# Loading the V cache in rows of 4 KB and the first weight in rows of 8 KB in a grouped-query decode attention kernel

**The chip, the cores and the metric.** The kernel runs on one core of a Trainium2 chip, with the other cores idle. The metric is the time of one execution on the device in microseconds; lower is better. A profiled execution also has a span, from its first to its last instruction, which is 1.7 to 3.0 us shorter than that execution's time in the runs of this case. Each run is classed as fast or slow by how far it lies above the fastest run of the same kernel; comparisons below use fast runs unless the text says otherwise.

## The reference, cut to what matters

```python
# x [32,1,512], k_cache and v_cache [32,8,2048,128], wq [512,4096], wo [4096,512], all bf16
W = 512                                            # only the last 512 keys count
q = (x @ wq) as [32, 32 heads, 1, 128]
k, v = the last W keys of each cache, each of 8 heads shared by 4 query heads
p = softmax(q @ k^T / sqrt(128)) ;  out = (p @ v) as [32, 4096] @ wo
```

Each of the 32 batch elements needs 1 MB of K and 1 MB of V, used once. With wq and wo, 4 MB each, 75.5 MB have to be read. A key of one head is 256 B, and the keys of a head follow each other in memory, so it is a choice of the kernel how many keys in a row go to one partition. The heads lie 512 KB apart, because the cache holds 2,048 keys of each.

## The kernel before

One queue issues all loads, in the order K0, wq, V0, K1, V1, ..., wo. A slot is a buffer for the K or the V of one batch element:

```python
def load_k(b):                 # 4 K slots; rows of 16 keys = 4 KB
    if b >= NK:
        sp.wait_ge(pe_T3, b - NK + 1)
    for h in range(2):
        sp.dma_start(
            K_sb[:, b % NK, h * 16 * DH:(h + 1) * 16 * DH],
            k_cache[b, 4 * h:4 * h + 4, SK - W:, :].rearrange("g (s r) d -> s g (r d)", s=32),
        ).then_inc(sem_k[b % NK][h], 16)

def load_v(b):                 # 12 V slots; rows of kt = 4 keys = 1 KB
    ...
    sp.dma_start(
        v_slot(b)[:, :, :],
        v_cache[b, :, SK - W:, :].rearrange("g (p kt) d -> p g (kt d)", kt=KT),
    ).then_inc(sem_v[b % NV], 16)
```

wq comes as four column blocks in rows of 2 KB, wo in rows of 1 KB. Per batch element TensorE transposes K in 32 pieces (line 253 of the kernel before), VectorE copies three quarters of the result out of PSUM, the memory that TensorE writes to (it evicts them), and ScalarE one, and eight products give the scores. Per four elements (a quad) there is one softmax, four transposes of P (line 283) and a burst of 128 products with V (line 303), in which 128 keys of one head are contracted with the four columns of that head:

```python
for g in range(G):
    for kt in range(KT):
        last = pe.matmul(
            QO_ps[:, j * 32 + 4 * g: j * 32 + 4 * g + 4],
            lhsT=v_slot(b)[:, g, kt * DH:(kt + 1) * DH],
            rhs=PT_sb[:, qq % 2, kt * 128 + prow(g, j): kt * 128 + prow(g, j) + 4],
            start=(kt == 0), stop=(kt == KT - 1), tile_position=(0, 0),
        )
```

At the end, 32 products with wo (line 332) are summed on four strips of the array, and one more product adds the strips.

## Time and profile before

| kernel before | |
|---|---|
| time | 216.6 us median of 3 runs (216.5 to 217.15) |
| span of the profiled run | 215.7 us (this run took 217.76 us, a little over the three) |
| busiest compute engine | TensorE, 149.2 us (69%) |
| queue of all loads | 99.4% of the 16 DMA engines' span |
| rate, 27 to 165 us | 376 GB/s |
| mean granted TensorE clock | 0.79 |

Read it like this: a queue that is never empty, and engines that are idle a third of the time, mean that bytes over rate set the time. The share of the DMA engines says only that they always have something in hand, not that they carry as much as they could (from 27 to 165 us it reads 1.06 at 376 GB/s here, and 1.03 at 408 after the change). The GB/s row tells how much.

### The profile page before, as it was taken

The numbers are of one execution on the slowest core, as the hardware profiler recorded it, in microseconds if no ns is written. First come the engines' busy times: TensorE is split into PE (matmuls) and PEld (weight loads), VectorE is DVE, ScalarE is ACT, GpSimd is POOL, SyncE is SP. The second block draws the span as 40 slices with busy tenths as digits, with TensorE's granted clock in tenths as the row PEclk, the third lists the DMA queues.
The fourth block names the chain that finished last, engine by engine and source line by source line (L and its number), as shares of the span: only waits on it lengthen the run. The fifth ranks groups of instructions, "written<-read, shape, count | busy, mean of one in ns | idle before, by whom it ended". The sixth has DMA issues, their size and how long they took to land.

```text
span 215.7 us, 5573 instructions
## 1 busy us (share of the span) xinstructions
PE 149.2 (69%) x2501; PEld 120.0 (56%) x2501; DVE 89.7 (42%) x141; ACT 46.3 (21%) x61; POOL 10.0 (5%) x45
## 2 busy tenths in 40 slices
PE   0175755648955897486948984689758795895672
PEld 0164635437843786376727953678438484783620
DVE  0044733460546154623463355515661366055112
ACT  2001120232113212320332031121331122213103
POOL 6000200000000000000000000000000000000000
PEclk9999596997598858985697679685997587859655
DMA  5999999999999999999999999999999999999910
GB/s 166 369 397 374 375 376 375 375 375 375 375 378 376 377 376 378 378 377 376 377 377 375 378 376 378 373 377 377 375 377 377 376 372 376 376 366 319 354 67 6
DMA packets 48886, 75.91 MB, mean 352 GB/s; under 512 B 1696, under 2 KB 38624, under 8 KB 48864
## 3 DMA queue, kind: packets, MB, share of 16 engines
q1 hardware_dynamic: 48864, 75.57, 99.4%
q8 instruction: 19, 0.31, 0.6%
q14 instruction: 3, 0.02, 0.0%
HBM read 75.53 MB, written 0.03 MB: 350 GB/s over the span
## 4 chain that ended last, share of the span: by engine, by line
DMA 41%; PE 34%; SPq 13%; issue 5%; ACT 4%; DVE 1%; DVEq 0%; ACTq 0%
DMA K_sb<-in_k_cache_dram 41%; PE KT_ps L253 18%; PE QO_ps L303 13%; SPq L138 10%; SPq L148 3%; ACT PT_sb L437 2%; PE KT_ps L332 2%; ACT KT_sb L420 2%; SPq L129 1%; PE S_ps L271 1%; DVE P_bf L379 0%; DVEq L43 0%; DVE oT_sb L387 0%; DVE maxv L369 0%; DVE X_sb L406 0%
## 5 line engine op out<-in xcount | busy, mean ns | idle before, releaser
L253 PE MATMUL KT_ps<-perm,K_sb 128*128 128x128 bf16 x1024 | 90.7, 266 | 39.5 <-DMA K_sb<-in_k_cache_dram 32.9
L253 PEld LDWEIGHTS KT_ps<-perm,K_sb 128*128 128x128 bf16 x1024 | 81.8, 123 | 56.1 <-DMA K_sb<-in_k_cache_dram 48.1
L363 DVE COPY KT_sb<-KT_ps 128x1024 bf16<-128x1024 bf16 x96 | 63.8, 690 | 50.2 <-PE KT_ps L253 49.0
L420 ACT ACTIVATE KT_sb<-KT_ps 128x1024 bf16<-128x1024 bf16 x32 | 32.8, 1024 | 148.7 <-PE KT_ps L253 148.7
L303 PEld LDWEIGHTS QO_ps<-PT_sb,V_sb 128*128 128x128 bf16 x768 | 20.3, 100 | 7.2 <-ACT PT_sb L437 7.2
L303 PE MATMUL QO_ps<-PT_sb,V_sb 128*128 128x4 bf16 x768 | 20.8, 165 | 4.4 <-ACT PT_sb L437 4.4
L271 PE MATMUL S_ps<-KT_sb,QBD 128*32 128x512 bf16 x256 | 23.3, 446 | 0.7 <-ACT KT_sb L420 0.7
L387 DVE CAST oT_sb<-QO_ps 128x128 bf16<-128x128 f32 x8 | 5.8, 719 | 40.3 <-PE QO_ps L303 40.3
L208 POOL COPY QBD<-QT_sb 128x32 bf16<-128x32 bf16 x32 | 6.3, 211 | 145.3 <-PE S_ps L271 128.2
L353 DVE CAST QT_sb<-QO_ps 128x512 bf16<-128x512 f32 x2 | 4.8, 2392 | 13.7 <-PE QO_ps L231 13.7
L231 PE MATMUL QO_ps<-xT_sb,big_sb 128*128 128x32 bf16 x128 | 4.0, 183 | 9.2 <-DMA big_sb<-in_wq_dram 9.2
L231 PEld LDWEIGHTS QO_ps<-xT_sb,big_sb 128*128 128x128 bf16 x128 | 3.8, 101 | 9.4 <-issue 7.4
L303 PEld LDWEIGHTS QO_ps<-PT_sb,big_sb 128*128 128x128 bf16 x256 | 6.8, 100 | 2.8 <-ACT PT_sb L437 2.8
L303 PE MATMUL QO_ps<-PT_sb,big_sb 128*128 128x4 bf16 x256 | 7.0, 165 | 1.8 <-ACT PT_sb L437 1.8
L271 PEld LDWEIGHTS S_ps<-KT_sb,QBD 128*32 128x32 bf16 x256 | 4.0, 98 | 5.4 <-issue 3.3
L369 DVE TENSOR_REDUCE maxv<-S_ps 128x1 f32<-128x512 f32 x8 | 5.5, 691 | 3.4 <-PE S_ps L271 3.4
L428 ACT ACTIVATE P_f<-S_ps,negmax 128x512 f32<-128x512 f32 x8 | 5.5, 687 | 4.5 <-DVE negmax L371 4.5
L379 DVE TENSOR_SCALAR P_bf<-P_f,recip 128x512 bf16<-128x512 f32 x8 | 5.9, 742 | 0.3
L283 PE MATMUL PT_ps<-ident,P_bf 128*128 128x128 bf16 x32 | 3.8, 255 | 2.8 <-DVE P_bf L379 2.8
L332 PE MATMUL KT_ps<-wo_sb,oT_sb 128*32 128x512 bf16 x32 | 4.2, 628 | 1.5 <-DVE oT_sb L387 0.8
L437 ACT ACTIVATE PT_sb<-PT_ps 128x512 bf16<-128x512 bf16 x8 | 4.7, 592 | 1.5 <-PE PT_ps L283 1.5
L283 PEld LDWEIGHTS PT_ps<-ident,P_bf 128*128 128x128 bf16 x32 | 2.7, 117 | 3.3 <-DVE P_bf L379 3.3
(27 smaller groups left out, 15.4 us busy)
## 6 DMA issues: line engine op xcount, KB each, us to landing
K_sb<-in_k_cache_dram SPq DMA_DIRECT2D x64, 512.0 KB, 11.2
V_sb<-in_v_cache_dram SPq DMA_DIRECT2D x24, 1024.0 KB, 11.8
big_sb<-in_v_cache_dram SPq DMA_DIRECT2D x8, 1024.0 KB, 11.7
big_sb<-in_wq_dram SPq DMA_DIRECT2D x4, 1024.0 KB, 10.7
wo_sb<-in_wo_dram SPq DMA_DIRECT2D x4, 1024.0 KB, 12.8
x_sb<-in_x_dram SPq DMA_DIRECT2D x1, 32.0 KB, 1.7
out_dram<-out_sb SPq DMA_DIRECT2D x1, 32.0 KB, 1.5
```

Source lines behind the costliest of these rows:

```text
L138: sp.dma_start(K_sb[:, b % NK, h * 16 * DH:(h + 1) * 16 * DH], k_cache[b, 4 * h:4 * h + 4, SK - W:, :].rearrange("g (s r) d -> s g (r d)", ...
L148: sp.dma_start(v_slot(b)[:, :, :], v_cache[b, :, SK - W:, :].rearrange("g (p kt) d -> p g (kt d)", kt=KT),).then_inc(sem_v[b % NV], 16)
L208: pool.tensor_copy(dst, src).then_inc(pool_qbd, 1)
L231: last = pe.matmul(QO_ps[:, hl * 32:(hl + 1) * 32], lhsT=wq_sb[:, kt, h * DH:(h + 1) * DH], rhs=xT_sb[:, kt, :], start=(kt == 0), stop=(kt ...
L253: last = pe.matmul(KT_ps[:, t, i * 128:(i + 1) * 128], lhsT=K_sb[:, b % NK, r * DH:(r + 1) * DH], rhs=perm[:, :, :], start=True, stop=True ...
L271: last = pe.matmul(S_ps[32 * (g % 4):32 * (g % 4) + 32, q % 2, :], lhsT=QBD[:, b % NQB, g, :], rhs=KT_sb[:, b % NKT, g // 4, :, g % 4, :], ...
L283: last = pe.matmul(PT_ps[:, kt * 128:(kt + 1) * 128], lhsT=P_bf[:, qq % 2, kt * 128:(kt + 1) * 128], rhs=ident[:, :], start=True, stop=Tru ...
L303: last = pe.matmul(QO_ps[:, j * 32 + 4 * g: j * 32 + 4 * g + 4], lhsT=v_slot(b)[:, g, kt * DH:(kt + 1) * DH], rhs=PT_sb[:, qq % 2, kt * 12 ...
L332: last = pe.matmul(KT_ps[:, c, :].bitcast(F32)[32 * c:32 * (c + 1), :], lhsT=oT_sb[:, h, :], rhs=wo_sb[:, h, :], start=(h < 4), stop=(h >= ...
L363: dve.tensor_copy(KT_sb[:, b % NKT, t // 2, 8 * (t % 2):8 * (t % 2) + 8, :, :], KT_ps[:, t, :]).then_inc(dve_T, 1)
L420: act.activation(KT_sb[:, b % NKT, t // 2, 8 * (t % 2):8 * (t % 2) + 8, :, :], KT_ps[:, t, :], ACTF.Copy).then_inc(act_T, 1)
L437: act.activation(PT_sb[:, qq % 2, :], PT_ps[:, 0:512], ACTF.Copy).then_inc(act_PT, 1)
```

## The change

The intent is to load V in rows of 4 KB too, and wq in rows of 8 KB. V then lies in the array like K: partition (s, g) holds 16 keys of key block s of head g, so four heads share one 128-row operand. P has to follow: the softmax is written into a zeroed tile in which the probabilities of a head stand only where its partitions are (block-diagonal), so that one product contracts 32 key blocks times four heads. It costs 16 transposes of P per quad in place of four, and four strided writes on VectorE in place of one. The diff, cut to its core:

```diff
-    NK = 4
-    NV = 12
+    NK = 6
+    NV = 8
+    LEAD = 5
+    PVLAG = 6
 ...
+        def cache_rows(cache, b, h):
+            return cache[b, 4 * h:4 * h + 4, SK - W:, :].rearrange("g (s r) d -> s g (r d)", s=NS)
 ...
+            for kt in range(DKT):
+                sp.dma_start(wq_sb[:, kt, :], wq[kt * P:(kt + 1) * P, :]).then_inc(sem_wq[kt], 16)
 ...
             def load_v(b):
                 if b >= NV:
-                    sp.wait_ge(pe_PV, quad_of(b - NV) + 1)
 ...
+                    sp.wait_ge(pe_PV, b - NV + 1)
+                for h in range(2):
+                    sp.dma_start(
+                        V_sb[:, b % NV, h].rearrange("p r d -> p (r d)"), cache_rows(v_cache, b, h)
+                    ).then_inc(sem_v[b % NV], 16)
+
+            for b in range(B + LEAD):
+                if b < B:
+                    load_k(b)
+                if b >= LEAD:
+                    load_v(b - LEAD)
 ...
-                    v_cache[b, :, SK - W:, :].rearrange("g (p kt) d -> p g (kt d)", kt=KT),
 ...
+                for c in range(G4):
+                    rows = slice(32 * c, 32 * c + 32)
+                    dve.tensor_scalar(
+                        P_ex[rows, :, :, c], P_f32[rows, :].rearrange("p (r s) -> p r s", r=NR),
+                        recip[rows, q:q + 1], None, op0=ALU.mult,
+                    ).then_inc(dve_P, 1)
 ...
+                for h in range(2):
+                    r0 = score_row(h, j)
+                    for r in range(NR):
+                        ins = pe.matmul(
+                            QO_ps[:, 16 * h:16 * h + 16],
+                            lhsT=V_sb[:, b % NV, h, r, :],
+                            rhs=PT_sb[:, q % 2, r, :].rearrange("p (c n) -> p c n", c=G4)[:, :, r0:r0 + 4],
+                            start=(r == 0), stop=(r == NR - 1), tile_position=(0, 0),
+                        )
```

The scores and P in f32 have one buffer in place of two, wo takes wq's place in memory, and V's products are done per element, six elements behind K. wq now comes before K0 in the queue.

## The prediction

> **What bounds the kernel now.** I read the page from the top, then the queue's own numbers, then the memory rate in chosen stretches, then the end of the chain. The first two parts of the page already name the bound.
>
> ```profile
> PE 149.2 (69%) x2501; PEld 120.0 (56%) x2501; DVE 89.7 (42%) x141; ACT 46.3 (21%) x61; POOL 10.0 (5%) x45
> ...
> PEclk9999596997598858985697679685997587859655
> DMA  5999999999999999999999999999999999999910
> GB/s 166 369 397 374 375 376 375 375 375 375 375 378 376 377 376 378 378 377 376 377 377 375 378 376 378 373 377 377 375 377 377 376 372 376 376 366 319 354 67 6
> DMA packets 48886, 75.91 MB, mean 352 GB/s; under 512 B 1696, under 2 KB 38624, under 8 KB 48864
> ...
> q1 hardware_dynamic: 48864, 75.57, 99.4%
> ```
>
> No compute engine is over 70% busy, while the 16 DMA engines read 9 in every slice from the second to the one before the tail. The rate is flat at 375 GB/s, and it has one hump, 397, in the slice in which mostly wq arrives. 75.57 MB have to come in whatever the order; the time is their number divided by the rate, plus a start and a tail. The packet line says how they come: nearly 38,600 of the 48,886 packets are under 2 KB. These are V (32 MB in 1 KB rows) and wo (4 MB in 1 KB rows); K comes in 4 KB rows, wq in 2 KB rows.
>
> Next question: does the row size matter, or is 375 what memory gives? The stretches' view (columns: stretch, its length, busy time of five engines, TensorE clock, DMA share, GB/s):
>
> ```profile
> 9.00:15.00 6.00, 3.25 (x78) 3.18 (x79) 1.16 (x1) 0.00 (x0) 0.00 (x0) 1.00 1.04 396
> 27.00:192.00 165.00, 123.50 (x2077) 101.21 (x2074) 74.67 (x122) 37.95 (x50) 5.07 (x24) 0.79 1.06 376
> 195.00:204.00 9.00, 4.82 (x122) 3.59 (x120) 3.23 (x7) 2.40 (x4) 0.00 (x0) 0.87 1.06 340
> ```
>
> With the DMA share at 1.04 to 1.06 in all three, the rate is 396 with wq in flight (2 KB), 376 with K and V mixed (half 4 KB, half 1 KB) and 340 with wo nearly alone (1 KB). To separate K from V in the middle I counted in the trace's packet records how many 1 KB and 4 KB packets start in each microsecond of 27 to 192 us and fitted a time per packet to each size: 2.93 ns for 1 KB and 10.17 ns for 4 KB, so 350 and 403 GB/s for the core. Half and half that gives 2/(1/350+1/403) = 375, the rate shown. So row size is what costs.
>
> Does compute limit it anywhere? The waits of TensorE (who waited for what, total us, times, longest us):
>
> ```profile
> PE KT_ps L253 <- DMA K_sb<-in_k_cache_dram: 32.9, 24, 3.4
> PE QO_ps L231 <- DMA big_sb<-in_wq_dram: 9.2, 3, 7.4
> PE QO_ps L303 <- ACT PT_sb L437: 6.2, 8, 0.9
> ```
>
> TensorE waits for K, not the reverse. The chain also has 9.6% at the K issues waiting for a free K slot, but as the queue stays full behind that wait, it is back-pressure and costs nothing. The end:
>
> ```profile
> 205.39 0.72 DVE oT_sb L387
> 206.16 0.62 PE KT_ps L332 x3
> 206.77 0.66 issue
> 207.43 3.61 PE KT_ps L332 x29
> 211.07 0.68 DVE X_sb L406
> ```
>
> The last softmax, transposes and 128 PV products (201.8 to 205.4) are done just before the last wo packet. In the packet records the full stream falls off at 204.6 us, but some of the 16 engines lag and the last wo byte lands at 208.4. From the last wo product (211.05) to the end of the span (215.7) it is 4.65 us.
>
> [...] the clock in the trace is indeed 0.50 or 1.00 in every stretch short enough to hold one state. [...] the 128 PV products with 4 columns took 3.47 us in the chain, 27 ns each, so 16 columns in place of 4 should be free.
>
> **The change, part by part.**
> 1. V in 4 KB rows (the core). 33.55 MB at 403 in place of 350 GB/s: 95.9 us become 83.3, so -12.6 us on the path, since the queue is the bound. It is the largest term.
> 2. wq in 8 KB rows, and first in the queue. 4.19 MB at 394 (fitted for 2 KB) becomes at least 403: -0.2 us. The projection moves later: the last quarter of wq lands at about 13 us, TensorE then does 32 products (1.0 us for 32 in the trace). Copies of the result and the first transposes finish by about 20 us. Six K slots and V0, 7 MB or 18 us of transfers, are already issued by then, so the queue should not run dry.
> 3. wo stays in 1 KB rows, in wq's place: 12.4 us at the 337 seen (mean rate for wo), unchanged. It waits for the projection, long done.
> 4. K has 6 slots in place of 4, V 8, freed one at a time; V's load lags by 5 and PV by 6. A K load needs the transposes of the batch element six earlier, at which point about five K and five V blocks (10 MB) are outstanding. No gap in the queue; no gain either, as it had none.
> 5. Compute per batch element. TensorE at full clock: 32 transposes (16 took 1.08 us) 2.16, 8 score products 0.62, 32 PV products 0.87, and 16 instead of 4 transposes of P per quad (1.08/4) 0.27: 3.9 us. At half clock 3.45 + 1.04 + 0.87 + 0.43 = 5.8 us. The transfer of 2.10 MB at 403 takes 5.2 us. VectorE: three evictions of 0.69, 2.07; max, negation and reciprocal (0.69+0.15+0.16)/4 = 0.25; four normalisations on 32 partitions with a stride, estimated at the 0.74 of the present one, 0.74; one small copy, estimated 0.15: 3.2 us. ScalarE: 1.02, plus (0.88 + 2 x 1.02)/4: 1.75 us. All lie beside the transfers.
> 6. The tail. V31 lands a whole wo before the end, 12 us early; softmax and PV end before wo does. All but the last eight wo products run as wo arrives; the trace has four in 0.43 us, so eight and the semaphore are about 1.0 us after the last byte, against 2.65 now (208.4 to 211.05): -1.6 us.
>
> Sum, built up: first bytes at 2.3 us; wq 10.4; K and V 67.11 MB at 403, 166.5; wo 12.4: the mean engine ends at 191.6. The same sum for before, 2.6 + 10.6 + 83.3 + 95.9 + 12.4 = 204.8, meets the observed 204.6. Slowest engine +3.5 (before: 3.8): 195.1. Eight products 1.0, then 4.65: a span of 200.8. The measured time is 0.9 over the span (216.6 against 215.7): 201.7. [...] I take 200.6.
>
> **Rivals.**
> a) TensorE becomes the bound. For: at half clock it needs 5.8 us a batch element against 5.2 for the transfers, and the mean granted clock before is 0.79. Against: [...] five elements of prefetch absorb a slow spell. Even at half clock all through, 32 x 5.8 + about 16 + a tail of 7 makes some 209.
> b) The 4 KB gain is not there when all the rows have the same 512 KB pitch between heads: 403 was fitted with V's 1 KB rows beside. Against it speaks that K's half has that pitch already. If the whole stream stayed at 376, the tail and wq alone would save 2 us: some 214.
> c) The single score buffer, the single P buffer and the order on VectorE stall TensorE: four normalisations (about 3 us) stand between evictions once per quad. TensorE has 1.3 us of slack per element and the lag of 6; I see no chain longer than a period: 200 to 203.
> d) The uneven engines: [...] the slowest may end later than +3.5: up to 204.
>
> **Range and chances.** The transfer sum matched before within 0.2 us, so the error is the 4 KB rate (395 to 410, -3 to +4 us) and the tail (2 us either way): 196.5 to 205.5. Faster by over 2% means under 212.3, which only rival b) in full prevents: 0.95; within 2% 0.03; slower 0.02, for a stall I don't see.
>
> **What would show it.** DMA share at 9 throughout, and the rate at 400 or more in the middle slices in place of 376; packets near 23,000, with those under 2 KB near 5,900; TensorE still waiting on K, clock above 0.79; PV products near 27 ns apart; the chain ending in wo's landing, eight products and the same 4.65 us. The prediction is wrong if slices fall below 390, if zeros appear in the DMA row, or if the chain runs through VectorE's normalisation or TensorE without DMA.

Its sum comes to a span of 200.8 us and a time of 201.7. A term for a faster stream of 4 KB rows alone followed, and the 1.1 us between 201.7 and the forecast of 200.6 were taken off for it. That 16 columns cost no more than 4 keeps a ground in the trace before: its products with 4 columns start 26 ns apart (median), and those with 32 columns in the projection (line 231) also 26.

## The result, and the profile after

The changed kernel takes 200.39 us (median of 4 runs, 200.34 to 200.56) against 216.88 us (216.5 to 217.87) in the runs beside it, and it is correct. A ratio here is the mean time of one kernel's fast runs over that of the other's in the same rounds, so it is not quite the ratio of the medians: 0.9235, with a 95% interval of 0.9201 to 0.9268. The span of the profiled runs fell from 215.7 to 198.7 us, by 17.0; the medians differ by 16.5, as the profiled run of the kernel before was one of its longer ones.

The page of the changed kernel, with the busy time of the engines, the slices, and the first queue:

```profile
PE 142.8 (72%) x2597; PEld 111.8 (56%) x2597; DVE 100.8 (51%) x188; ACT 58.3 (29%) x70; POOL 13.3 (7%) x46
...
PEclk9999999699999969988998799969996797855555
DMA  5999999999999999999999999999999999999930
GB/s 181 424 418 411 409 407 412 403 411 407 408 411 403 409 407 407 410 407 409 406 407 410 407 413 403 408 407 407 411 406 411 401 409 406 410 396 334 344 133 7
DMA packets 23289, 75.95 MB, mean 382 GB/s; under 512 B 2208, under 2 KB 6368, under 8 KB 22752
```

The DMA row reads 9 as before, but the same row now stands for 401 to 413 GB/s in the middle and not for 375. The packets have halved. VectorE has become busier (51%), ScalarE too, and neither matters. Two stretches (same columns as in the prediction) show the rates of the two row sizes, wq at the start and K with V in the middle:

```profile
5.00:14.00 9.00, 3.56 (x113) 3.27 (x114) 0.00 (x0) 0.00 (x0) 1.30 (x4) 1.00 1.01 422
27.00:165.00 138.00, 109.44 (x2021) 86.69 (x2019) 84.36 (x157) 47.69 (x56) 6.01 (x22) 0.91 1.03 408
```

What TensorE waited for (total us, times, longest us):

```profile
PE KT_ps L236 <- DMA K_sb<-in_k_cache_dram: 22.4, 32, 1.6
PE PT_ps L268 <- DVE P_ex L359: 10.6, 6, 3.1
PE PT_ps L214 <- DMA w_sb<-in_wq_dram: 7.6, 4, 3.4
PE KT_ps L308 <- DMA w_sb<-in_wo_dram: 6.0, 4, 1.9
```

It still waits for K, now 32 short times, and for wo at the end. The second line is new: the block-diagonal writes hold up the transposes of P. Whether that costs anything can't be read from this view alone; an experiment below asks. The end of the chain:

```profile
181.61 11.21 DMA w_sb<-in_wo_dram
...
192.86 1.11 PE KT_ps L308 x8
...
194.00 0.68 DVE X_sb L382
```

Before, the chain reached wo's products through VectorE's copy of the last quad and did 32 of them in a row. Now it comes straight from the last wo transfer, and eight products are left.

The packet records (every packet of a trace, with its start, duration and size) give the span's bookkeeping, by when so many bytes had landed:

| stretch | before | after | gain |
|---|---|---|---|
| until 4.3 MB have landed (wq, some K) | 14.31 us | 13.08 us | 1.23 |
| the next 67.1 MB (about K and V) | 178.44 | 164.43 | 14.01 |
| until the last byte of wo | 15.64 | 14.85 | 0.79 |
| from there to the last product of wo | 2.66 | 1.61 | 1.05 |
| from there to the end of the span | 4.65 | 4.73 | -0.08 |
| sum | 215.7 | 198.7 | 17.0 |

### The profile page after: what moved, and what is told of

The parts are those of the page before. It is cut to its first block, busy times and chain, and to the rows that moved or that the text cites. A ratio compares the mean times of both kernels' runs of the same rounds, so it can differ in the third digit from the quotient of the medians.

```text
span 198.7 us, 5891 instructions
## 1 busy us (share of the span) xinstructions
PE 142.8 (72%) x2597; PEld 111.8 (56%) x2597; DVE 100.8 (51%) x188; ACT 58.3 (29%) x70; POOL 13.3 (7%) x46
## 4 chain that ended last, share of the span: by engine, by line
SPq 50%; DMA 28%; PE 14%; DVE 3%; issue 2%; ACT 1%; DVEq 0%
SPq L132 24%; DMA K_sb<-in_k_cache_dram 23%; SPq L140 18%; PE KT_ps L236 9%; SPq L151 7%; DMA w_sb<-in_wo_dram 6%; PE S_ps L253 2%; DVE P_ex L359 2%; PE QO_ps L286 1%; SPq L126 1%; DVE KT_sb L337 1%; PE PT_ps L268 1%; PE KT_ps L308 1%; ACT P_f L407 0%; DVEq L45 0%
## 5 line engine op out<-in xcount | busy, mean ns | idle before, releaser
L236 PE MATMUL KT_ps<-perm,K_sb 128*128 128x128 bf16 x1024 | 75.8, 238 | 22.6 <-DMA K_sb<-in_k_cache_dram 22.4
L236 PEld LDWEIGHTS KT_ps<-perm,K_sb 128*128 128x128 bf16 x1024 | 67.0, 107 | 29.2 <-DMA K_sb<-in_k_cache_dram 26.7
L286 PEld LDWEIGHTS QO_ps<-PT_sb,V_sb 128*128 128x128 bf16 x1024 | 28.2, 98 | 17.4 <-issue 13.9
L286 PE MATMUL QO_ps<-PT_sb,V_sb 128*128 128x16 bf16 x1024 | 31.2, 171 | 2.4 <-ACT PT_sb L417 1.2
L359 DVE TENSOR_SCALAR P_ex<-P_f,recip 32x512 bf16<-32x512 f32 x32 | 25.3, 791 | 1.1
L417 ACT ACTIVATE PT_sb<-PT_ps 128x1024 bf16<-128x1024 bf16 x16 | 15.5, 1021 | 19.1 <-PE PT_ps L268 19.1
L268 PE MATMUL PT_ps<-ident,P_ex 128*128 128x128 bf16 x128 | 9.7, 236 | 10.6 <-DVE P_ex L359 10.6
L268 PEld LDWEIGHTS PT_ps<-ident,P_ex 128*128 128x128 bf16 x128 | 8.2, 106 | 11.5 <-DVE P_ex L359 11.5
L366 DVE CAST oT_sb<-QO_ps 128x32 bf16<-128x32 f32 x32 | 5.9, 183 | 9.5 <-PE QO_ps L286 9.4
L308 PE MATMUL KT_ps<-w_sb,oT_sb 128*32 128x512 bf16 x32 | 4.3, 637 | 6.0 <-DMA w_sb<-in_wo_dram 6.0
```

The costliest lines, as they stand in the source:

```text
L236: ins = pe.matmul(KT_ps[:, t, i * 128:(i + 1) * 128], lhsT=K_sb[:, b % NK, h, 8 * (t % 2) + i, :], rhs=perm[:, :, :], start=True, stop=Tru ...
L268: ins = pe.matmul(PT_ps[:, r // 8, (r % 8) * 128:(r % 8 + 1) * 128], lhsT=P_ex[:, r, :, :].rearrange("p s g -> p (s g)"), rhs=ident[:, :], ...
L286: ins = pe.matmul(QO_ps[:, 16 * h:16 * h + 16], lhsT=V_sb[:, b % NV, h, r, :], rhs=PT_sb[:, q % 2, r, :].rearrange("p (c n) -> p c n", c=G ...
L359: dve.tensor_scalar(P_ex[rows, :, :, c], P_f32[rows, :].rearrange("p (r s) -> p r s", r=NR), recip[rows, q:q + 1], None, op0=ALU.mult,).th ...
L417: act.activation(PT_sb[:, q % 2, 8 * i:8 * i + 8, :].rearrange("p r n -> p (r n)"), PT_ps[:, i, :], ACTF.Copy,).then_inc(act_PT, 1)
```

## The experiments

All twelve ran on chips with the kernel before beside them. Five were made to ask about the gain, two about the tail, and five about whether rows can be made longer still, a question that the 422 GB/s of wq raised.

**Undo V's rows alone.** V is loaded as before, and the result is wrong:

```diff
-                for h in range(2):
-                    sp.dma_start(... cache_rows(v_cache, b, h)).then_inc(sem_v[b % NV], 16)
+                sp.dma_start(
+                    V_sb[:, b % NV].rearrange("p h r d -> p (h r d)").rearrange("p (g x) -> p g x", g=G),
+                    v_cache[b, :, SK - W:, :].rearrange("g (p kt) d -> p g (kt d)", kt=4),
+                ).then_inc(sem_v[b % NV], 16)
```

> The changed kernel with one part undone: V is loaded as in the kernel before, one transfer of 1 MB in 1 KB rows (the result is wrong on purpose, since the key order no longer matches). Theory (the row size of V is the gain): 33.55 MB at 350 in place of 408 GB/s cost 13.6 us, so 214 us, with the middle of the run at 376 GB/s. Rival (the gain comes from six K slots, the lag and the new order of work): within 2 us of 200.4. Mixed: in between, in proportion.

Measured: 214.47 us (214.36 to 214.53). The middle of this run, in the stretches' view:

```profile
27.00:165.00 138.00, 104.98 (x1856) 83.61 (x1856) 77.02 (x144) 43.67 (x52) 5.71 (x22) 0.89 1.06 376
```

The rate is back at 376 GB/s with all of the new slots, lag and order of work in place. The rival falls.

**V's rows alone, in the kernel before.** The other direction, wrong too:

```diff
-                sp.dma_start(v_slot(b)[:, :, :],
-                    v_cache[b, :, SK - W:, :].rearrange("g (p kt) d -> p g (kt d)", kt=KT))
+                for h in range(2):
+                    sp.dma_start(
+                        v_slot(b).rearrange("p g f -> p (g f)")[:, h * 2048:(h + 1) * 2048],
+                        v_cache[b, 4 * h:4 * h + 4, SK - W:, :].rearrange("g (s r) d -> s g (r d)", s=32))
```

> The kernel before with the one part alone: V loaded in 4 KB rows by two transfers of 512 KB (wrong on purpose, the products of V are those of the kernel before). Theory: 13.6 us less than 216.9, so 203, with 408 GB/s in the middle. Rival (the four K slots and the bursts of 128 products of the kernel before can't keep a faster stream fed): over 208, with the rate in the middle under 395.

Measured: 203.35 us (203.12 to 204.44), ratio 0.9363. The middle:

```profile
27.00:165.00 138.00, 111.01 (x1842) 90.11 (x1839) 65.99 (x108) 34.17 (x45) 5.03 (x24) 0.78 1.03 408
```

The old compute, with four K slots, feeds the faster stream just as well. So the way in which V is loaded accounts for 14.0 us of the span when taken away from the new kernel (212.7 against 198.7) and 14.2 when given to the old one (215.7 against 201.5); in median times it is 14.1 both ways. The 2.8 us of span that are left between this kernel and the changed one come from its start (0.95 us, by when 4.3 MB have landed) and its tail: its last product of wo ends 3.48 us after wo's last byte, and the changed kernel's 1.61.

Both runs change the order of V's addresses and the number of its transfers together with the row size, so the order could be a rival. Two records speak for the row size itself. The run with wq in 1 KB rows, below, leaves the addresses in memory as they are. And in the packet records of these kernels the most common duration of a packet is 46 ns for 1 KB (V before, wo), 84 for 2 KB (wq before), 159 for 4 KB (K, and V after) and 309 for 8 KB (wq after). These four lie on one line: 37.6 ns for every KB and 8.4 ns for each packet. Four packets of 1 KB thus take 1.16 times as long as one of 4 KB.

**Four K slots in place of six.**

```diff
-    NK = 6
+    NK = 4
```

> The changed kernel with four K slots in place of six, all else unchanged and the result right. Theory (depth has no part in the gain): within 0.6 us of 200.4. Rival (depth keeps the queue full): 203 or more, with gaps in the rate.

Measured: 200.49 us (200.46 to 200.52), correct; the span is 198.6. The depth of the K buffer has no part in the gain.

**wq in 1 KB rows.**

```diff
-                sp.dma_start(wq_sb[:, kt, :], wq[kt * P:(kt + 1) * P, :])
+                sp.dma_start(
+                    w_sb[:, 8 * kt:8 * kt + 8, 0:D], wq[kt * P:(kt + 1) * P, :].rearrange("p (a n) -> p a n", a=8))
```

(w_sb becomes 32 rows of 528 elements, so that pieces of 1 KB don't touch.)

> The changed kernel with wq in 1 KB rows (weights held in a padded tile, so that a row of wq falls into eight pieces), result right. Theory (the rate follows the row size for every input and the queue is the bound from the first byte): 4.19 MB at 350 in place of 424 GB/s, 2.1 us more, 202.5. Rival (the start is not on the path, as compute has to catch up anyhow): within 0.5 us of 200.4.

Measured: 202.63 us (202.51 to 202.78), correct, span 200.9. The start of this run:

```profile
5.00:14.00 9.00, 3.08 (x96) 2.79 (x96) 0.00 (x0) 0.00 (x0) 1.29 (x4) 1.00 1.09 361
```

361 GB/s in place of 422, and the 2.2 us of span that it costs stay in the sum to the end. The start is on the path. Only the length of the pieces differs here on the side of memory, and 422 over 361 is 1.17, as 408 over the fitted 350 for V is.

**Compute alone.** K and V are loaded until the slots are full, and then used again (wrong):

```diff
                 if b >= NK:
-                    sp.wait_ge(pe_T[3], b - NK + 1)
+                    return
 ...
                 if b >= NV:
-                    sp.wait_ge(pe_PV, b - NV + 1)
+                    return
```

> The changed kernel with only the first six K and eight V blocks loaded and then used again and again, so the transfers end early and all compute stays (wrong on purpose). Theory (transfers bound the kernel, compute has slack): 14 us of start, 32 elements at about 4 to 4.6 us and a tail of some 20 us: 160 to 180. Rival (TensorE or VectorE are within a few per cent of the bound too): 190 or more.

Measured: 171.44 us median; the runs are 169.53 to 172.27. TensorE's waits begin with:

```profile
PE PT_ps L268 <- DVE P_ex L359: 15.3, 8, 3.1
```

So the block-diagonal writes do stall TensorE, once in every quad, by 15.3 us in all, and this is part of what compute needs. But compute needs about 170 us in all, 30 below the changed kernel; this run's own loads were over after about 63 us. An element takes 4.2 us in it (1,623 products from 60 to 150 us, at 32+32+8+4 = 76 per element), and a transfer of 2.10 MB at 408 GB/s takes 5.1. The stall lies beside the transfers: V's rows alone in the kernel before, without these writes, gave the same 408 GB/s.

**The tail: V last.** All of wo is loaded before the last four V blocks:

```diff
             for b in range(B + LEAD):
 ...
+                for c in {24: [0], 25: [1], 26: [2], 27: [3]}.get(b - LEAD, []):
+                    load_wo(c)
```

> The changed kernel with all of wo loaded before the last four V blocks, so V31 lands last; result right. Theory (the tail behind the last byte is on the path): PV of the last element 1.0, its copy 0.2 and 32 products of wo at 1.07 per eight, 5.5 us in place of 1.6 behind the last byte: 3.9 more, less what the freer queue gives, 202.5 to 204.5. Rival (the tail does not matter): 200.4 within 0.5.

Measured: 205.82 us (205.16 to 206.05), correct: above the range that I had expected. The chain's end shows the mechanism:

```profile
193.23 1.02 PE QO_ps L289 x32
...
194.52 3.66 PE KT_ps L311 x32
```

V's last byte landed at 192.61 us and the last product of wo ended at 198.18, 5.6 us behind it in place of 1.6. The span, 202.7, is 4.0 us over that of the changed kernel, as the tail says. The time is 2.5 to 3.0 us above the span here, against 1.7 to 1.8 for the changed kernel, and that is what took it over the range. The kernel before (1.8 to 3.0 in the rounds of the experiments, mostly over 2.4) and the run with V's rows alone (2.5 to 2.9) have this too; what the three share is not shown.

**wo spread among the last V loads.** As above, with `{27: [0], 29: [1], 31: [2, 3]}`.

> The changed kernel with wo's first two loads moved between the last V loads (after V27 and V29), two left at the end; result right. In the changed kernel the issue of wo's last two transfers waits 12 us and the rate falls to 308 GB/s with a DMA share of 0.94 there. Theory (fast engines run dry while the issue waits for room): 1 to 2 us less, 199. Rival (1 KB rows and the slowest engine set the time wherever wo lies): 200.4 within 0.5.

Measured: 200.32 us (200.01 to 200.55), ratio 0.9203, interval 0.9175 to 0.9232, correct. The theory falls. From 180 to 190 us the rate is now 349 GB/s, but the last byte of wo lands at 192.32 us, and in the changed kernel it was 192.36. The bytes of wo merely moved; the last of them lands when it did. This is the nearest that any run came to beating the changed kernel, and it does not.

**Longer rows: K and V in 8 KB rows.** wq had shown 422 GB/s, so I tried 8 KB for all, with one transfer of 1 MB each (wrong):

```diff
-                        K_sb[...], cache_rows(k_cache, b, h)            # [32 blocks][4 heads][4 KB], twice
+                    K_sb[:, b % NK].rearrange("p h r d -> p (h r d)"),  # [16 blocks][8 heads][8 KB], once
+                    k_cache[b, :, SK - W:, :].rearrange("g (s r) d -> s g (r d)", s=16),
```

> The changed kernel with K and V each loaded by one transfer of 1 MB in 8 KB rows (wrong on purpose). Theory (a fixed cost per row): wq's stretch in 8 KB rows showed 424 GB/s, so 67.1 MB go from 164.5 to 158.3 us and the time to 194. Rival (4 KB is already at the ceiling and wq's 424 only showed a fresh queue): within 1 us of 200.4.

Measured: 317.54 us (307.05 to 318.93). Both expectations were far off. The DMA and GB/s rows of its page:

```profile
DMA  7999999999999999999999999999999999999990
GB/s 278 354 222 224 226 225 225 225 224 226 230 230 230 230 226 228 233 230 234 231 240 238 254 257 261 259 267 258 260 249 263 274 266 253 254 249 231 242 317 24
```

The engines are as busy as ever, at 222 to 274 GB/s in the middle. Four more kernels changed one thing of the pattern each. All vary by several per cent from run to run, and the lowest run stands in the table. The rates of the five slow patterns are those of the profiled runs; the gap to 408 GB/s is far larger than the differences among runs of a kernel.

| blocks x heads x row of a transfer | blocks taken together | lowest run | GB/s, 50 to 150 us |
|---|---|---|---|
| 32 x 4 x 4 KB (the changed kernel) | all | 200.34 us | 408 |
| 16 x 8 x 8 KB | all | 307.05 | 229 |
| 16 x 4 x 8 KB, on 64 partitions | all | 305.51 | 228 |
| 16 x 8 x 4 KB | every other | 282.42 | 244 |
| 16 x 8 x 4 KB | adjacent ones | 263.95 | 250 |
| 16 x 4 x 4 KB, on 64 partitions | adjacent ones | 296.05 | 255 |

The edits and expectations, in that order. Four heads in rows of 8 KB:

```diff
-            return cache[b, 4 * h:4 * h + 4, SK - W:, :].rearrange("g (s r) d -> s g (r d)", s=NS)
+            return cache[b, 4 * h:4 * h + 4, SK - W:, :].rearrange("g (s r) d -> s g (r d)", s=16)
```

> K and V in 8 KB rows again, but each 512 KB transfer fills 64 partitions from 16 blocks of four heads in place of 128 partitions from 16 blocks of eight (wrong on purpose). Theory A (a row of 8 KB out of heads that lie 512 KB apart is slow in itself): near 317 us and 225 to 245 GB/s as with eight heads. Theory B (the eight heads of the pattern did it): 200 us or less.

Median 312.87 us: not the eight heads alone. Rows of 4 KB in the pattern of the slow run:

```diff
+            return cache[b, :, SK - W:, :].rearrange("g (s h r) d -> h s g (r d)", s=16, h=2)[h]
```

> K and V in 4 KB rows, but fetched in the pattern of the slow 8 KB run: each 512 KB transfer takes the first or second half of 16 blocks of all eight heads, 8 KB apart (wrong on purpose). Theory A (row length of 8 KB): about 200 us with 400 GB/s or more. Theory B (pattern of eight heads at 512 KB distance): over 250 us.

Median 295.1 us: not the row length alone. Adjacent blocks in place of every other one:

```diff
+            return cache[b, :, SK - W:, :].rearrange("g (h s r) d -> h s g (r d)", s=16, h=2)[h]
```

> As the slow run in 4 KB rows of eight heads, with one difference: a transfer takes 16 blocks that follow each other in memory (the first or the second half of a head's window) in place of every other block (wrong on purpose). Theory (blocks fetched side by side that leave every other 4 KB out are what is slow): about 200 us and 400 GB/s or more. Rival (eight heads in one transfer are what is slow): 280 us or more, as before.

Median 281.14 us: not the gaps, or not they alone. The last one is correct and puts the same bytes in the same places in rows of 4 KB; each transfer of the changed kernel is only cut in two:

```diff
+            for i in range(2):
+                sp.dma_start(
+                    K_sb[64 * i:64 * i + 64, b % NK, h].rearrange("p r d -> p (r d)"),
+                    cache_rows(k_cache, b, h, i))      # keys 256*i to 256*i + 255, s=16
```

> The changed kernel with each 512 KB transfer of K and V cut into two of 256 KB, over the first and the last 16 blocks of the same four heads: rows of 4 KB, the same bytes in the same places, result right. All four slow patterns so far had 16 blocks per transfer. Theory A (16 blocks per head in a transfer are what is slow): 260 us or more. Theory B (eight heads side by side, or 8 KB rows of four heads, are what is slow): 200 to 204, the extra being eight issues of about 0.6 us per element in a period of 5.1.

Median 305.49 us (296.05 to 306.09), as theory A expected:

```profile
DMA  6999999999999999999999999999999999999990
GB/s 267 376 241 242 243 245 251 248 262 259 260 262 253 256 248 250 251 258 259 259 259 263 255 248 246 248 245 245 240 240 240 241 243 247 253 248 246 297 309 13
```

The queue is full throughout, so the doubled number of issues is not what holds it up. The packet records show where the time goes: from 50 to 150 us a packet of 4 KB takes 262 ns (median) in place of 161 in the changed kernel, while wq's packets of 8 KB take 309 ns as ever. What the five slow patterns share is an outermost dimension of 16 on the side of memory, where the fast loads have 32 (K, V) or 128 (wq, the old V). That is a correlation over five kernels. The profile doesn't name the engine that carried a packet. Why a packet of such a transfer takes longer stays open, and so does what 8 KB rows of the caches would give in a pattern with more blocks.

## Why the prediction was right, point by point

The time was predicted as 200.6 us, with a range of 196.5 to 205.5; it is 200.39. The mechanism and the place of the bound were right. The figure was closer than its terms, some of which erred in opposite directions, so part of its closeness is luck (see "From span to time").

- **V's rows (step 1).** Predicted -12.6 us; both experiments say -14, in either direction. The fit to the mixed stream had put 4 KB at 403 GB/s, and the stream runs at 408 once all of it is in 4 KB rows, so K gained a little as well (the median packet of 4 KB from 27 to 165 us took 164 ns before and 161 after). K and V took 164.4 us in place of the 166.5 of the sum.
- **wq (step 2).** Predicted -0.2 us, taken with a cautious "at least 403" for 8 KB. It is mis-sized: the start gained 1.23 us, because 8 KB rows gave 422 against 392 to 396 GB/s in 2 KB rows, and the first row starts 0.4 us earlier (2.23 us against 2.61). That the queue would not run dry behind the later projection held: no slice dips.
- **wo (step 3).** The stretch was to be unchanged at 12.4 us plus 3.5 for the slowest engine. It took 14.85 in place of 15.9.
- **Depth (step 4).** No gain, as said; the run with four slots shows it.
- **Compute (step 5).** Beside the transfers, as said. The estimates were 3.9 us per element for TensorE at full clock, and compute alone needed 4.2 with the stalls. A normalisation on 32 partitions took 0.79 us against 0.74 assumed, the small copy 0.18 against 0.15. The 16-column products start 25 to 26 ns apart within a burst, and those with 4 columns in the kernel before 26: free, as said. (A burst of 32 lasts 0.95 to 1.02 us, but that includes the 169 ns of its last product, so it is not to be divided by 32.)
- **The tail (step 6).** Predicted -1.6 us, measured -1.05: it is 1.6 us from the last byte to the last product, and not 1.0, as half a microsecond passes before the first of the eight products starts. The order is worth more than that figure says: beside a fast stream, the old tail would have been 3.5 us, and with V last it is 5.6.
- **From span to time.** I added 0.9 us, but this was the median time of three runs (216.6) less the span of another: the run with the span of 215.7 us took 217.76, so the difference was 2.1 before. In the changed kernel it was 1.7. The span (198.7) came out 2.1 us under the sum (200.8). The 0.8 us that I added too little, and the 1.1 us by which I had gone below my own 201.7, made up for nearly all of that. In the rounds of the experiments the difference was 2.6 us in the median for the kernel before, so some 0.8 us of the gain in time lies outside the span; no term of the sum has it, and its cause is not known.
- **The rivals.** a), TensorE as the bound: its clock rose from 0.79 to 0.87, and compute alone ends 30 us earlier, with TensorE busy for 91% of the stretch from 60 to 150 us at a clock of 0.91. b), no gain from 4 KB when all of K and V has one pitch: refuted by 408 GB/s. Yet its worry was sound in kind: the experiments show address patterns that cut the rate to 244 to 255 GB/s at the same row length. c), stalls on VectorE: they exist (10.6 us, six times) and cost nothing while transfers are the bound. d), uneven engines: 16 packets or more are in flight until 189.1 us and the last byte of wo lands at 192.4, 3.3 us later; before it was 3.7 us (204.7 to 208.4). In that time the share of the 16 engines falls by steps, from 0.77 (189 to 190 us) over 0.56 and 0.27 to 0.06, and before from 0.52 (205 to 206 us) over 0.32 and 0.16 to 0.03. So the slowest is no later than before, and the 3.5 us of the sum hold.

## What to carry to other kernels

When a DMA queue is always busy and no engine is, look at the GB/s beside the busy share, fit a time per row size, and multiply: the row size of V was worth 14 of 17 us of the span here, and the extra transposes and writes were free beside it. Put last in the queue what has the least work behind it, as the work behind the last byte was added whole here (5.6 us of it in place of 1.6 made the span 4.0 us longer). And measure a pattern before building on it: rows twice as long, or the same rows in transfers cut in half, made this kernel take about half as long again.
